# Q left unscaled before the score matmul, the scale inside the exponential, and the exponential's bias and the threshold made by one vector operation on two columns

## The chip, the cores and the metric

The kernel runs on one core of a Trainium2 chip. The metric is the device time of one execution in microseconds (us), the median of several runs; less is better. A core has TensorE (PE; PEld is its weight load), VectorE (DVE), ScalarE (ACT), GpSimd (POOL) and SyncE (SP), which issues most DMAs. Each engine takes its instructions in the order in which they are written and waits for others through semaphores.

## The reference

Sparse attention, then a layer of eight experts with one expert per token, then a dense layer with a gate:

```
scale = 1/sqrt(64);  scores = scale * q @ k.T           # 4 batches, 8 heads, 576 positions, 64 wide
thresh = max(scores) - tau                              # per query, tau = 0.02
scores = where(scores >= thresh, scores, -1e9)
attn = exp(scores - max(scores)); attn /= sum(attn) + 1e-9
x = (attn @ v), heads side by side                      # 2304 tokens x 512
e = argmax(x @ w_gate); x = gate * relu(x @ w1[e]) @ w2[e]
h = x @ w_in; out = (h * sigmoid(1.702 h)) @ w_out      # 512 -> 2048 -> 512
```

All tensors are float32.

## The kernel before, in words

**Stages.** Attention runs to about 303 us, the experts from there to 572 us, the dense layer to the end. In the last part of attention the expert with most tokens already starts on 256 tokens, which are known before the last queries are done.

**Attention.** The queries are cut into ten units: eight of 256 queries (two chunks of 128) and two "remainder" units of 2 x 64 queries of two batches. A tile is 128 queries by one head by 576 keys: 16 tiles in a full unit, 8 in a remainder unit, 144 in all. For each tile:

1. PE (`s_mm`, L360) multiplies Q by K. Both are float32 values split into a high part and a low part in the PE's reduced float format: Q as `qh` and `ql`, K as two halves of the 128 rows. The scores go to `pair`, two PSUM banks; there are three pairs. Columns 0 to 287 of both banks are used.
2. DVE (`red`, L370) makes the negated maximum `nm` of the 576 scores.
3. ACT (`thresh`, L374) makes the threshold `thr` = maximum - tau, one column.
4. ACT (`expo`, L378) makes `et` = exp(scores + nm).
5. DVE (`stt`, L389) makes `pt` = (scores >= thr) * et, with its row sum. This frees the pair.
6. PE transposes `pt` (L405; L416 for the remainder of the keys), ACT copies it to `ptT` (L411, L420), and PE multiplies it by V (L432, L442).

At the end of a unit, ACT copies its output to `aoT` (L451), PE brings it back and makes the router's logits (L478), DVE finds the maximum and its index (`lw`, `lg`, `mx`, `mi`), POOL makes the one-hot rows `oh` (L551, L553), PE counts with them (L602 to L605), and POOL scatters the tokens' numbers to their expert's table (L641).

**Q and K.** Q arrives by DMA as `qraw`. Apart from the first two of the 40 pieces, POOL handles each of its 38 pieces of 128 x 512 with three operations: it multiplies by the scale in place (`sc`, L306), makes `qh` (L318), and makes `ql` = Q - `qh` (L325). K goes through two (L282, L285), where one half of the rows gets the high part and the other the low part.

**Order.** The program is not written in a fixed order. Each piece of work is an `op` with an engine, a cost and a key (from the table `KEYS` and the tile's number); a planner (`Plan.order`) repeatedly takes the operation that can start first by its costs, the one with the lowest key among equals, and writes it out. So an edited operation, cost or key can reorder every engine.

**The first expert.** When unit 7 of 0 to 9 has been counted (the last of them that is needed for the 256 tokens), `pick_ops` finds the largest expert, SP reads its number into a register and loads its weights (`wraw`), POOL splits them (L770, L776), POOL gathers the 256 rows (L1229, `xg`), PE transposes these (L802), ACT and DVE split them (L807, L811), and PE starts on the expert (L1243).

## Time and profile before

| | us |
|---|---|
| timed runs | 977.53, 977.88, 980.33; median 977.88 |
| the profiled execution, whole | 984.31 |
| its span, first to last instruction | 982.6 |
| busy in the span: PE, DVE, ACT, POOL | 954.6, 562.9, 529.7, 411.2 |
| attention, to the first matmul of the first expert | 303.3 |
| experts, to the first matmul of the dense layer | 572.3 |

PE is busy for 97% of the span and its granted clock is 0.987 of full speed on average. A busy PE is not a PE at its peak: matmuls are pipelined, and a row's duration contains the pipeline's fill. So in the rows below the distance from one start to the next says more than the duration.

### The profile page before, as it was taken

Reading aid. Unit: us, or ns where it says so; the run is one execution under the profiler, and the core shown is the slowest. Engines: PE = TensorE matmul, PEld = TensorE weight load, DVE = VectorE, ACT = ScalarE, POOL = GpSimd, SP = SyncE. Lnnn points to the kernel's source line nnn. Section 1 sums busy time; section 2 is a strip of 40 time slices with the busy share of each in tenths; the row PEclk is TensorE's granted clock in tenths of the full one; section 3 lists DMA queues with packets and bytes.
Section 4 is the critical chain, followed back from the end, with each engine's and each line's share of the span. In section 5 each row is a group of like instructions: output and inputs, shape, how many; then the busy total and the mean of one; then the engine's idle time right before and its main releaser. Section 6 shows DMA issues by size and latency. Waiting matters only on the chain.

```text
span 982.6 us, 16924 instructions
## 1 busy us (share of the span) xinstructions
PE 954.6 (97%) x6204; PEld 864.9 (88%) x6205; DVE 562.9 (57%) x1189; ACT 529.7 (54%) x1170; POOL 411.2 (42%) x455
## 2 busy tenths in 40 slices
PE   7998999999989899999999999999999999999996
PEld 5888888888879899999999998999999999999995
DVE  6886888888856347888995488882411111111111
ACT  5886889889854345766675465543322322322221
POOL 6979978845275213555450000001432422522321
PEclk7999999999989999999999999999999999999999
DMA  8723532300243567877776373300200100000000
GB/s 309 223 88 109 162 108 79 108 22 22 58 137 108 171 197 217 257 214 235 241 223 212 116 220 86 106 24 13 95 22 1 54 11 1 33 0 1 33 1 33
DMA packets 50551, 106.90 MB, mean 109 GB/s; under 512 B 12816, under 2 KB 22032, under 8 KB 49936
## 3 DMA queue, kind: packets, MB, share of 16 engines
q1 hardware_dynamic: 45632, 93.43, 30.4%
q0 software_dynamic: 4096, 11.56, 3.8%
q8 instruction: 50, 0.82, 0.4%
q10 hardware_dynamic: 736, 0.79, 0.2%
q14 instruction: 37, 0.30, 0.1%
HBM read 87.37 MB, written 18.57 MB: 108 GB/s over the span
## 4 chain that ended last, share of the span: by engine, by line
PE 61%; DVE 2%; DMA 2%; issue 1%; ACT 0%; POOLq 0%; SPq 0%; DVEq 0%; ACTq 0%
PE b L1639 21%; PE b L1666 20%; PE b L1259 12%; PE b L1243 9%; DVE wlo L1393 1%; DMA wraw<-in_w 1%; PE b L1234 1%; DMA out<-xg,ids 1%; DVE hl L1250 0%; ACT whi L1389 0%; POOLq L1883 0%; DVE wil L1172 0%; ACT xg L1671 0%; ACT yt L1504 0%; ACT hh L1247 0%
## 5 line engine op out<-in xcount | busy, mean ns | idle before, releaser
L1648 DVE SCALAR_TENSOR_TENSOR th<-th,b 128x384 f32<-128x384 f32 x96 | 53.1, 553 | 250.1 <-ACT th L1644 250.1
L1644 ACT ACTIVATE th<-b 128x384 f32<-128x384 f32 x96 | 47.2, 492 | 201.9 <-PE b L1639 198.8
L1639 PE MATMUL b<-x2h,wil 128*128 128x384 f32 x384 | 129.5, 337 | 0.0
L1639 PE MATMUL b<-x2h,wih 128*128 128x384 f32 x384 | 129.3, 337 | 0.0
L1639 PE MATMUL b<-x2l,wih 128*128 128x384 f32 x384 | 128.9, 336 | 0.0
L370 DVE TENSOR_REDUCE nm<-pair 128x1 f32<-128x576 f32 x144 | 107.0, 753 | 27.8 <-PE pair L360 26.2
L389 DVE SCALAR_TENSOR_TENSOR pt<-pair,thr,et 128x576 f32<-128x576 f32 x144 | 114.3, 813 | 13.3 <-ACT et L378 12.3
L1659 POOL TENSOR_TENSOR gl<-th,gh 128x384 fp32r<-128x384 f32 x60 | 61.0, 1017 | 140.1 <-ACT gh L1656 136.3
L1666 PE MATMUL b<-woh,gl 128*128 128x512 f32 x276 | 109.2, 396 | 0.0
L1666 PE MATMUL b<-wol,gh 128*128 128x512 f32 x276 | 109.0, 395 | 0.0
L1666 PE MATMUL b<-woh,gh 128*128 128x512 f32 x276 | 107.3, 389 | 0.0
L378 ACT ACTIVATE et<-pair,nm 128x576 f32<-128x576 f32 x144 | 107.3, 745 | 0.0
L411 ACT COPY ptT<-bank 128x512 f32<-128x512 f32 x144 | 81.3, 589 | 25.4 <-PE bank L405 25.1
L1393 DVE TENSOR_TENSOR wlo<-wraw,whi 128x1024 fp32r<-128x1024 f32 x56 | 75.9, 1375 | 27.1 <-ACT whi L1389 24.1
L405 PE MATMUL bank<-ident,pt 128*128 128x128 f32 x576 | 86.1, 283 | 4.3 <-DVE pt L389 3.3
L1623 POOL TENSOR_TENSOR x2l<-xr,x2h 128x384 fp32r<-128x384 f32 x16 | 16.1, 1033 | 170.5 <-ACT x2h L1619 170.5
L360 PE MATMUL pair<-kst,qh 128*128 128x288 f32 x320 | 84.9, 348 | 1.3 <-DVE kst L285 0.6
L405 PEld LDWEIGHTS bank<-ident,pt 128*128 128x128 f32 x576 | 68.5, 145 | 17.3 <-ACT thr L374 6.2
L1639 PEld LDWEIGHTS b<-x2h,wih 128*128 128x128 f32 x384 | 72.2, 188 | 4.2 <-DVE th L1648 0.3
L1639 PEld LDWEIGHTS b<-x2l,wih 128*128 128x128 f32 x384 | 72.1, 188 | 3.9
L1639 PEld LDWEIGHTS b<-x2h,wil 128*128 128x128 f32 x384 | 72.0, 188 | 0.0
L1259 PE MATMUL b<-hh,whi 128*128 128x448 f32 (+6 forms) x224 | 71.4, 319 | 0.1
(256 smaller groups left out, 2309.6 us busy)
## 6 DMA issues: line engine op xcount, KB each, us to landing
wraw<-in_w SPq DMA_DIRECT2D x64, 512.0 KB, 4.7
qraw<-in_qd SPq DMA_DIRECT2D x40, 256.0 KB, 4.0
wiraw<-in_wi SPq DMA_DIRECT2D x32, 256.0 KB, 4.0
wraw<-in_wo SPq DMA_DIRECT2D x16, 512.0 KB, 3.6
kraw<-in_kd SPq DMA_DIRECT2D x14, 576.0 KB, 4.6
vt<-in_vf SPq DMA_DIRECT2D x4, 1024.0 KB, 7.6
xn<-xt SPq DMA_DIRECT2D x16, 256.0 KB, 3.2
xr<-x2t SPq DMA_DIRECT2D x20, 192.0 KB, 2.7
```

Of the source, the lines that this page charges most:

```text
L360: nc.tensor.matmul(s_ps[:, n, 0:288], w, ks[bb][:, h, 288 * n : 288 * n + 288], start=(i == 0), stop=(i == len(seq) - 1),)
L370: nc.vector.tensor_reduce(t["nm"], t["s"][:, :, 0:288], axis=AX.XY, op=ALU.max, negate=True)
L378: nc.scalar.activation(t["e"], t["s"][:, :, 0:288], AF.Exp, bias=t["nm"], scale=1.0)
L389: nc.vector.scalar_tensor_tensor(pt[:, 576 * x : 576 * x + 576].rearrange("p (n k) -> p n k", n=2), t["s"][:, :, 0:288], t["thr"][:, 0:1], ...
L405: nc.tensor.transpose(t["t"][:, c, :], pt[:, o : o + 128], ident)
L411: nc.scalar.copy(blk["ptT"][:, 4 * x : 4 * x + 4, 128 * ci : 128 * ci + 128], t["t"])
L1243: self.nc.tensor.matmul(h_ps, ww[:, o : o + 128], xx[dc], start=(k == 0), stop=(k == 11))
L1259: self.nc.tensor.matmul(y_ps, w[:, o : o + 128], h, start=(k == 0), stop=(k == 23))
L1393: nc.vector.tensor_tensor(w[1], self.raws.pop((r, which, k)), w[0].bitcast(F32), op=ALU.subtract)
L1639: self.nc.tensor.matmul(h_ps, w[:, dc, :], x[:, dc, :], start=(k == 0), stop=(k == 11))
L1659: eng.tensor_tensor(self.g[n][1], self.th.pop(n), self.g[n][0].bitcast(F32), op=ALU.subtract)
L1666: self.nc.tensor.matmul(o_ps, g[:, cs], w, start=(F == 0 and k == 0), stop=(F == 15 and k == 2))
```

## The change

Q is no longer multiplied by the scale 1/8. So the 38 operations `sc` on POOL go, and the scores in PSUM are eight times the reference's. The scale is put into the exponential: exp(scale * scores + bias), with bias = scale * `nm`. The threshold becomes maximum - 8 tau. Bias and threshold are now the two columns of one tile `thr`, made by one DVE operation per tile: (two constants) times `nm` plus (two constants). The first pair of constants, 1/8 and -1, stands in columns 500 and 501 of each PSUM pair, where no matmul writes; the second, `btadd`, in SBUF. ACT's operation `thresh` goes, and ACT's `expo` now waits for `thr` and not for `nm`. At the start DVE writes the constants (12 small operations in place of 2). The values in `KEYS` are different, so the planner writes another order.

```diff
 KEYS = dict(
-    KF=24.61, S=-3.65, R=61.35, X=43.87, TH=43.74, ST=85.35, T=-82.22, TE=40.03, TR=-1.15, TRE=-75.9, AV=1.41,
+    KF=-77.05, S=-4.92, R=-1.51, X=39.19, TH=-75.73, ST=24.75, T=-50.51, TE=74.0, TR=-50.68, TRE=-64.66, AV=0.13,
...
     def tau_prep():
         nc.vector.tensor_scalar(qscale, tau_sb, 0.0, float(D) ** -0.5, op0=ALU.is_ge, op1=ALU.mult)
-        nc.vector.scalar_tensor_tensor(ntau, tau_sb, -1.0, tau_sb, op0=ALU.mult, op1=ALU.min)
-
-    d_tau = pl.op("DVE", 0.3, -20, tau_prep, [dma(-200, 0.1, [tau_load])])
+        nc.vector.memset(btadd, 0.0)
+        nc.vector.tensor_scalar(ntau, tau_sb, 0.0, -3e38, op0=ALU.is_lt, op1=ALU.mult)
+        nc.vector.scalar_tensor_tensor(btadd[:, 1:2], tau_sb, -float(D) ** 0.5, ntau, op0=ALU.mult, op1=ALU.add)
+        for p in pairs:
+            nc.vector.memset(p[:, 0, 501:502], -1.0)
+            nc.vector.tensor_copy(p[:, 0, 500:501], qscale)
...
-        def sc():
-            q = qraws[ui][:, hs]
-            nc.gpsimd.tensor_scalar(q, q, qscale[:, 0:1], 0.0, op0=ALU.mult, op1=ALU.add)
...
             if fast:
-                nc.scalar.activation(h, q, AF.Copy, scale=qscale[:, 0:1])
-            elif pool:
+                nc.scalar.copy(h, q)
+            else:
                 nc.gpsimd.tensor_scalar(h, q, 1.0, 0.0, op0=ALU.mult, op1=ALU.add)
...
-        if pool:
-            o = pl.op("Pool", 0.7, key, sc, [o, d_tau])
...
     def thresh(t):
-        t["thr"] = sm_p.tile([128, 1], F32, name="thr")
-        nc.scalar.activation(t["thr"], t["nm"], AF.Identity, bias=ntau[:, 0:1], scale=-1.0)
+        t["thr"] = sm_p.tile([128, 2], F32, name="thr")
+        nc.vector.scalar_tensor_tensor(
+            t["thr"], t["s"][:, 0, 500:502], t["nm"][:, 0:1], btadd, op0=ALU.mult, op1=ALU.add
+        )
 
     def expo(t):
         t["e"] = e_p.tile([128, 2, 288], F32, name="et")
-        nc.scalar.activation(t["e"], t["s"][:, :, 0:288], AF.Exp, bias=t["nm"], scale=1.0)
+        nc.scalar.activation(t["e"], t["s"][:, :, 0:288], AF.Exp, bias=t["thr"][:, 0:1], scale=qscale[:, 0:1])
...
-                x = pl.op("ACT", 0.63, n + K["X"], lambda t=t: expo(t), [r], take=("e", te))
-                th = pl.op("ACT", 0.19, n + K["TH"], lambda t=t: thresh(t), [r])
-                deps = [x, th]
+                th = pl.op("DVE", 0.16, n + K["TH"], lambda t=t: thresh(t), [r, d_tau])
+                x = pl.op("ACT", 0.63, n + K["X"], lambda t=t: expo(t), [th], take=("e", te))
+                deps = [x]
```

What the planner makes of it is shown at three places. The first is POOL where unit 1 ends (about 80 to 89 us before). Before, with `oh` the one-hot rows for which PE waits:

```order
L306 TENSOR_SCALAR qraw<-qraw,qscale 128x512 x2
L318 TENSOR_SCALAR qh<-qraw 128x512 x2
L325 TENSOR_TENSOR ql<-qraw,qh 128x512 x2
L306 TENSOR_SCALAR qraw<-qraw,qscale 128x512 x5
L551 CAST ef<-mi 128x2
L553 TENSOR_SCALAR oh<-shc,ef 128x8 x2
```

And POOL there in the changed kernel (its line numbers are 2 lower in this part; L289 and L292 are the two operations on K):

```order
L289 TENSOR_SCALAR kst<-kraw,half 128x1152 x2
L292 TENSOR_TENSOR kst<-kraw,kst 128x1152 x2
L321 TENSOR_SCALAR qh<-qraw 128x512
L289 TENSOR_SCALAR kst<-kraw,half 128x1152
L325 TENSOR_TENSOR ql<-qraw,qh 128x512
L549 CAST ef<-mi 128x2
L551 TENSOR_SCALAR oh<-shc,ef 128x8 x2
```

The five scalings of Q that stood ahead of `oh` are gone; pieces of K for a later batch stand there in their place.

The second place is PE in the last units, where the first gathered rows are transposed (L802). Before, in the middle of the last unit's scores:

```order
L360 MATMUL pair_147<-kst,qh 128x288 x2
L360 MATMUL pair_147<-kst,ql 128x288 x2
L802 MATMUL bank_150<-ident,xg 128x128 x4
L405 MATMUL bank_149<-ident,pt 128x128 x4
L360 MATMUL pair_146<-kst,qh 128x288 x2
L360 MATMUL pair_146<-kst,ql 128x288 x2
```

In the changed kernel (L800 there), with the last products with V (L430, L440) and the first expert's matmul (L1241) around it:

```order
L800 MATMUL bank_149<-ident,xg 128x128 x4
L800 MATMUL bank_150<-ident,xg 128x128 x4
L476 MATMUL pair_146<-iw,aoT 128x144
L430 MATMUL pair_148<-ptT,vt 64x64 x8
L440 MATMUL pair_148<-ptT,vt_1429 128x64
L430 MATMUL pair_148<-ptT,vt 64x64 x8
L440 MATMUL pair_148<-ptT,vt_2234 128x64
L1241 MATMUL bank_149<-kraw,qraw 128x256 x12
```

Both transposes now stand behind all scores, a few matmuls ahead of the expert that reads them.

The third place is DVE in the steady part of attention. Before, with `pt` the masking of a tile:

```order
L370 TENSOR_REDUCE nm<-pair_147 128x1
L370 TENSOR_REDUCE nm<-pair_146 128x1
L389 SCALAR_TENSOR_TENSOR pt,sums<-pair_147,thr,et 128x576
L370 TENSOR_REDUCE nm<-pair_148 128x1
L370 TENSOR_REDUCE nm<-pair_147 128x1
L389 SCALAR_TENSOR_TENSOR pt,sums<-pair_146,thr,et 128x576
```

And in the changed kernel (L366 is the maximum there, L370 the new operation, L387 the masking):

```order
L366 TENSOR_REDUCE nm<-pair_148 128x1
L370 SCALAR_TENSOR_TENSOR thr<-pair_148,nm,btadd 128x2
L387 SCALAR_TENSOR_TENSOR pt,sums<-pair_146,thr,et 128x576
L387 SCALAR_TENSOR_TENSOR pt,sums<-pair_148,thr,et 128x576
L366 TENSOR_REDUCE nm<-pair_146 128x1
L366 TENSOR_REDUCE nm<-pair_147 128x1
L370 SCALAR_TENSOR_TENSOR thr<-pair_146,nm,btadd 128x2
L370 SCALAR_TENSOR_TENSOR thr<-pair_147,nm,btadd 128x2
```

One small operation per tile joins the two large ones, often right behind the maximum that it reads. Behind attention, the rows of PE, DVE, ACT and POOL are the same in both kernels, one for one; only some of SP's loads change places.

## Rows read from the trace of the kernel before

**Rows 1.** Stretches: length, busy of PE, PEld, DVE, ACT, POOL; clock, DMA, GB/s.
```profile
80.00:104.00 24.00, 21.08 (x246) 19.51 (x245) 15.11 (x41) 15.48 (x42) 22.68 (x28) 0.93 0.45 126
104.00:262.00 158.00, 157.39 (x1244) 131.05 (x1244) 138.98 (x348) 141.45 (x354) 108.04 (x139) 1.00 0.23 76
262.00:303.00 41.00, 37.02 (x363) 32.78 (x361) 28.34 (x61) 26.52 (x65) 26.12 (x24) 0.92 0.46 135
331.00:572.00 241.00, 237.78 (x1619) 233.42 (x1620) 173.03 (x310) 140.15 (x275) 83.71 (x85) 1.00 0.68 211
```

**Rows 2.** The chain that ended last: start, length, what.
```profile
331.27 2.27 PE b L1243 x14
...
572.29 8.32 PE b L1639 x48
```

**Rows 3.** Groups by line, 0 to 300 us: busy, mean ns | idle before, releaser.
```profile
L370 DVE TENSOR_REDUCE nm<-pair 128x1 f32<-128x576 f32 x144 | 107.0, 753 | 27.8 <-PE pair L360 26.2
...
L325 POOL TENSOR_TENSOR ql<-qraw,qh 128x512 fp32r<-128x512 f32 x38 | 48.1, 1276 | 0.2
L374 ACT ACTIVATE thr<-nm,ntau 128x1 f32<-128x1 f32 x144 | 44.5, 309 | 7.7 <-DVE nm L370 7.5
L285 POOL TENSOR_TENSOR kst<-kraw,kst 128x1152 fp32r<-128x1152 f32 (+1 forms) x15 | 38.5, 2569 | 0.0
...
L306 POOL TENSOR_SCALAR qraw<-qraw,qscale 128x512 f32<-128x512 f32 x38 | 25.9, 688 | 10.0 <-DMA qraw<-in_qd 9.8
L318 POOL TENSOR_SCALAR qh<-qraw 128x512 fp32r<-128x512 f32 x38 | 23.3, 622 | 6.9 <-PE pair L360 6.7
...
L282 POOL TENSOR_SCALAR kst<-kraw,half 128x1152 fp32r<-128x1152 f32 (+1 forms) x15 | 17.9, 1196 | 2.9 <-PE pair L360 2.4 <-DMA kraw<-in_kd 0.4
```

**Rows 4.** The same view, 104 to 262 us alone.
```profile
L374 ACT ACTIVATE thr<-nm,ntau 128x1 f32<-128x1 f32 x87 | 27.0, 311 | 1.0 <-DVE nm L370 0.9
```

**Rows 5.** Waits of the weight loads, 104 to 262 us: total, times, longest.
```profile
PEld bank L405 <- ACT thr L374: 4.2, 11, 0.4
```

**Rows 6.** Order of time on DVE: start, length, instruction; small operations on PSUM.
```profile
294.19 0.15 DVE L622 SCALAR_TENSOR_TENSOR rj<-bank,oh 128x8 f32<-128x8 f32 x1
...
294.27 0.16 DVE L622 SCALAR_TENSOR_TENSOR rj<-bank,oh 128x8 f32<-128x8 f32 x1
```

**Rows 7.** Order of time on POOL, the end of unit 1.
```profile
83.73 2.69 POOL L306 TENSOR_SCALAR qraw<-qraw,qscale 128x512 f32<-128x512 f32 x4
87.17 0.69 POOL L306 TENSOR_SCALAR qraw<-qraw,qscale 128x512 f32<-128x512 f32 x1 [0.74 <-DMA qraw<-in_qd]
```

**Rows 8.** Order of time on PE, the same place.
```profile
88.45 0.17 PE L602 MATMUL pair<-oh,tri 128*128 128x8 bf16 x1 [1.90 <-POOL oh L553]
```

**Rows 9.** Stretches behind two waits of PE, columns as in Rows 1.
```profile
88.45:94.25 5.80, 5.71 (x60) 5.49 (x59) 3.45 (x11) 0.93 (x4) 5.52 (x10) 0.71 0.28 99
279.25:285.80 6.55, 6.55 (x33) 5.18 (x35) 3.01 (x6) 2.92 (x6) 6.47 (x4) 0.56 0.37 113
```

**Rows 10.** Order of time on POOL: the first gather for the first expert.
```profile
274.39 1.02 POOL L1229 DMA_INDIRECT xg<-xn,itf  x1 [0.16 <-issue]
```

**Rows 11.** Order of time on PE around their transposes.
```profile
275.07 0.43 PE L360 MATMUL pair<-kst,ql 128*128 128x288 f32 x2
279.25 1.09 PE L802 MATMUL bank<-ident,xg 128*128 128x128 f32 x4 [3.75 <-DMA xg<-xn,itf]
...
301.70 0.61 PE L802 MATMUL bank<-ident,xg 128*128 128x128 f32 x4
```

**Rows 12.** Order of time on DVE, the first expert's second weights.
```profile
295.15 1.22 DVE L776 TENSOR_TENSOR kst<-wraw,kst 128x1024 fp32r<-128x1024 f32 x1
...
297.48 5.35 DVE L776 TENSOR_TENSOR kst<-wraw,kst 128x1024 fp32r<-128x1024 f32 x1 [0.36 <-ACT kst L772]
```

**Rows 13.** Order of time on POOL, beside the second of these.
```profile
299.38 2.35 POOL L776 TENSOR_TENSOR kst<-wraw,kst 128x1024 fp32r<-128x1024 f32 x1
```

**Rows 14.** Order of time on DVE, the first tiles.
```profile
9.66 1.18 DVE L327 SCALAR_TENSOR_TENSOR ql<-qraw,qscale,qh 128x512 fp32r<-128x512 f32 x1
```

More of the change, by code (lines that the diff above doesn't have):

```diff
@@ L182 @@
 KEYS = dict(
-    KF=24.61, S=-3.65, R=61.35, X=43.87, TH=43.74, ST=85.35, T=-82.22, TE=40.03, TR=-1.15, TRE=-75.9, AV=1.41,
-    OE=49.75, L=-76.58, F=53.56, FR=-35.48, FX=62.99, FS=16.49, K=28.16, Q=59.94, LD=11.03, P=22.54,
+    KF=-77.05, S=-4.92, R=-1.51, X=39.19, TH=-75.73, ST=24.75, T=-50.51, TE=74.0, TR=-50.68, TRE=-64.66, AV=0.13,
+    OE=71.86, L=6.66, F=85.05, FR=-35.13, FX=18.93, FS=77.49, K=49.92, Q=72.42, LD=20.32, P=109.57,
 )
@@ L263, in tau_prep @@
         nc.vector.tensor_scalar(qscale, tau_sb, 0.0, float(D) ** -0.5, op0=ALU.is_ge, op1=ALU.mult)
-        nc.vector.scalar_tensor_tensor(ntau, tau_sb, -1.0, tau_sb, op0=ALU.mult, op1=ALU.min)
-    d_tau = pl.op("DVE", 0.3, -20, tau_prep, [dma(-200, 0.1, [tau_load])])
+        nc.vector.memset(btadd, 0.0)
[4 more added lines that the diff above has]
+            nc.vector.tensor_copy(p[:, 0, 500:501], qscale)
+    btadd = cst.tile([128, 2], F32, name="btadd")
+    d_tau = pl.op("DVE", 1.2, -20, tau_prep, [dma(-200, 0.1, [tau_load])])
     def k_ops(b, h0, n, after, fast, key, first=None):
@@ L315, in hi @@
             if fast:
-                nc.scalar.activation(h, q, AF.Copy, scale=qscale[:, 0:1])
-            elif pool:
+                nc.scalar.copy(h, q)
+            else:
                 nc.gpsimd.tensor_scalar(h, q, 1.0, 0.0, op0=ALU.mult, op1=ALU.add)
-            else:
-                nc.gpsimd.tensor_scalar(h, q, qscale[:, 0:1], 0.0, op0=ALU.mult, op1=ALU.add)
         def lo():
             q, h, l = qraws[ui][:, hs], qs[ui][0][:, hs].bitcast(F32), qs[ui][1][:, hs]
-            if pool:
-                nc.gpsimd.tensor_tensor(l, q, h, op=ALU.subtract)
-            else:
-                nc.vector.scalar_tensor_tensor(l, q, qscale[:, 0:1], h, op0=ALU.mult, op1=ALU.subtract)
+            (nc.gpsimd if pool else nc.vector).tensor_tensor(l, q, h, op=ALU.subtract)
         pool = not fast and QPOOL[ui]
         o = dma(key + K["LD"] if first is None else first, 0.9, [load], after_raw)
-        if pool:
-            o = pl.op("Pool", 0.7, key, sc, [o, d_tau])
-        o = pl.op("ACT" if fast else "Pool", 0.6 if fast else 0.63, key, hi, [o, d_tau] + after_q)
+        o = pl.op("ACT" if fast else "Pool", 0.6 if fast else 0.63, key, hi, [o] + after_q)
         qop[(ui, g)] = pl.op("Pool" if pool else "DVE", 1.3 if pool else 0.68, key, lo, [o])
@@ L391, in stt @@
             t["s"][:, :, 0:288],
-            t["thr"][:, 0:1],
+            t["thr"][:, 1:2],
             t["e"],
```

## The prediction

> **What bounds the kernel now.** I read the page first (PE busy 97%, no other engine above 58%), then the chain of waits, the stretches, the groups by line, the waits, and last the order of time at the places where PE stood still. In the chain the reader is to see that from 331 us to the end it runs through PE matmuls with few other steps [rows 2], and the stretch to 572 us has PE busy for 237.8 of 241 us [rows 1]. The change leaves the order of PE, DVE, ACT and POOL behind attention as it was. So whatever attention gains or loses should come out at the end nearly one for one, and the question is how long attention takes.
>
> Attention has two kinds of stretches. From 104 to 262 us PE is busy for 157.4 of 158 us at full clock, beside an ACT that is busy for 141.5 and a DVE for 139.0 [rows 1]: PE is the bound, though not by much. From 80 to 104 us and from 262 to 303 us PE is idle for 2.9 and 4.0 us, and its granted clock is 0.93 and 0.92 [rows 1]. There the time is lost to single waits.
>
> **The change part by part.**
>
> *The threshold off ACT.* It removes 144 operations on ACT, busy for 44.5 us in all [rows 3]. PE bounds the long stretch, so this is worth only what PE waits for there. PE's idle time there is 0.6 us [rows 1]; the weight loads name an ACT threshold as the releaser for 4.2 us [rows 5], most of which lies beside matmuls still running. The gain is thus between 0 and 4.2 us.
>
> *One operation more per tile on DVE.* The trace has no such operation. The nearest is `rj`, also a scalar-tensor-tensor operation on a few PSUM columns: 0.15 to 0.16 us, and the next DVE operation starts 0.08 us after it started [rows 6]. From above I take the threshold on ACT, 0.309 us [rows 3], for the case that it is held up behind the maximum that it reads. The 158 us hold 87 of the 144 thresholds [rows 3, 4]. With 0.08 us DVE's 139.0 us become 146.0; with 0.16 us, 152.9; both less than 158, so PE stays the bound and the cost is nothing. With 0.309 us they become 165.9, 7.9 us over, and over all 144 tiles 7.9 x 144/87 = 13.1 us. I take 0.16 us, the row that is nearest in kind.
>
> For the steady part, gain and cost together, I take -1.5 us: near the 0.6 us of idle time in 158, a little more because ACT has 87 x 0.309 = 27 us less to do there, and the range is -4.2 to +13.1.
>
> *The scaling of Q off POOL.* It removes 38 operations of 0.688 us, 25.9 us [rows 3]. POOL is not the bound, but at one place PE waits for it: at 88.45 us PE has waited 1.90 us for the one-hot rows of unit 1 [rows 8], and these stand on POOL behind five scalings that begin at 83.73 and, with a wait for the last one's DMA, end at 87.86 [rows 7]. These are exactly the operations that go. Behind that wait PE's granted clock is 0.71 for 5.80 us [rows 9]: 5.80 x 0.29 = 1.7 us. I take both: -3.6 us.
> What is late next there: in the new order two high and two low parts of K, a piece of Q and one more high part of K stand ahead of the one-hot rows, 3 x 1.20 + 2 x 2.57 + 0.62 + 1.28 = about 10.6 us [rows 3], and with the one-hot rows themselves, by their time now, 11.5. They may start when the last scores of batch 0 are done. In PE's new order about 15 us of work (my count at the durations of such groups in the trace) stand between those scores and the count. That covers it by 3.5 us; if POOL comes late to that point, up to the 3.6 us return.
>
> *The transposes of the gathered rows.* PE ends its scores at 275.5 us and waits 3.75 us, until 279.25, for the first gather [rows 11], which POOL began at 274.39 [rows 10]. The granted clock is then 0.56 for 6.55 us [rows 9]: 6.55 x 0.44 = 2.9 us. In the new order both transposes stand behind all scores, as the second one does already now, at 301.70, with no wait [rows 11]. So the first wait goes with its slow clock: -6.65 us. It costs nothing that they come later as long as the split of the gathered rows is done in time. PE has about 2 us of work between the second transpose and the expert, and the split takes about as long.
>
> *The tail.* The split of the gathered rows stands on DVE behind the low part of the expert's second weights. That operation takes 1.22 us at one time and 5.35 us at another [rows 12], and the long one ends, at 302.83, only behind its neighbour on POOL, which ends at 301.73 [rows 13]. Before, PE was busy elsewhere during it. Now it would lie ahead of the split, and the loss is between 0 and 4.1 us. I take +1.0: it depends on which POOL operation stands beside it, and POOL's order there has gaps. The Trainium skill ("GPSIMD Engine Reference", section "1. Specifications") says that POOL's SBUF interfaces are shared with DVE, with contention for DVE operations with two SBUF inputs, as this one is. By that rule the loss is the full 4.1 us whenever POOL is at work, and the sum would be 3.1 us higher.
>
> *The start.* DVE writes 10 more constants between 3 and 5 us, while it waits for K. Then the first exponential has to wait for `thr`, which stands behind a low part of Q of 1.18 us [rows 14], and three thresholds join the maxima ahead of the first masking: 3 x 0.16 = +0.5 us (0 to 1.2).
>
> *The sum.* -1.5 - 3.6 - 6.65 + 1.0 + 0.5 = -10.25 us. The profiled execution took 984.31 us whole, 1.7 more than its span, and would take 974.1. The median of the timed runs is 977.88, 6.4 less than that execution; for the timed runs I predict 977.88 - 10.25 = 967.6 us.
>
> **The rivals.**
>
> *DVE becomes the bound in the steady part.* DVE reaches PE's 158 us when the operation takes (158 - 139)/87 = 0.22 us per tile, and the kernel gets slower than before from 0.28 us, where the loss of 8.75 us over 144 tiles eats the other terms. At 0.309 us: -10.25 + 1.5 + 13.1 = +4.4, 982.2 us. For it: it reads what the operation just ahead writes, DVE is already at 88%, and every wait of an engine at 97% is passed on. Against it: [rows 6], and other work often stands between the two. 11%.
>
> *The waits come back elsewhere.* POOL reaches the one-hot rows late (+3.6), or DVE's low part of the weights delays the expert (+3.1 beyond the 1.0), or another wait of a few us with its slow clock appears in the new order of the last units, for example because the first expert's weights, which start with the count of unit 7, now have six tiles fewer of PE's work before they are needed. Two of these: about +8, 975.6 us. For it: the old order too was a planner's, and had such waits. Against it: the loads of these weights have over 10 us to spare before. 20%.
>
> *PE gets all it can.* The steady part gives the whole 4.2 us, the tail and the start cost nothing: -14.45, 963.4 us. For it: ACT loses a fifth of its work. Against it: PE idles for 0.6 us only. 7%.
>
> **How the numbers follow.** The forecast, 967.6 us, has 62%, with a range of its own of 963 to 973. About 0.3%, 2.9 us, is what a measurement of this kernel can tell from no change: 975.0 to 980.8 counts as the same. Faster: 58 of the forecast's 62, 7 of the third rival, 7 of the second's 20, together 0.72. The same: 4 of the forecast, 11 of the second, 1 of the first, 0.16. Slower: 10 of the first, 2 of the second, 0.12. The range that should hold the time 8 times in 10 is 959.5 to 978.5: it takes in the second and the third rival, and leaves out the first and a little at the bottom.
>
> **What the new profile would show.** Right: no wait of PE over 1 us at the end of unit 1 and none at the transposes; a granted clock of 1.00 in the stretches that hold them; first expert matmul at about 293 us; a unit of 16 tiles at 29 us or a little less; the new operation at 0.15 to 0.17 us; DVE at about 96% in the steady part. Wrong: PE idle in the steady part with DVE's masking or ACT's exponential as the releaser (the first rival); PE waiting for the one-hot rows, for the split of the gathered rows or for the first expert's weights (the second); or attention shorter by 10 us and the end not, which would mean that the experts' loads and not attention set the time.

## The result, and the profile after

The changed kernel takes 988.20 us, median of 6 runs (987.02 to 989.26), beside 981.08 us for the kernel before on the same chip (977.53 to 982.78): ratio 1.0074, 95% interval 1.0046 to 1.0103. It is 7.1 us slower; forecast were 10.25 us less. The two profiled executions, 988.62 and 984.31 us, differ by 4.3 us only, since that of before was a long one. A second profiled execution took 979.76 us (before) and 990.29 us (after).

Where the difference lies is read off the same events in the traces (us, differences worked out from them; the last three columns are the second executions):

| from | to | before | after | difference | before, 2nd | after, 2nd | difference |
|---|---|---|---|---|---|---|---|
| start of the span | 57th masking | 125.5 | 122.2 | -3.3 | 122.7 | 122.5 | -0.2 |
| 57th masking | 129th masking (72 tiles of the steady part) | 130.5 | 135.1 | +4.6 | 130.5 | 135.2 | +4.7 |
| 129th masking | last masking | 40.4 | 31.0 | -9.3 | 39.0 | 31.0 | -7.9 |
| last masking | first matmul of the first expert | 7.0 | 15.6 | +8.6 | 7.0 | 18.9 | +11.8 |
| first expert | first matmul of the dense layer | 268.8 | 273.4 | +4.6 | 268.4 | 271.6 | +3.1 |
| dense layer | end | 410.5 | 409.5 | -1.0 | 410.5 | 409.5 | -0.9 |

In the new order the last masking stands earlier, so its two rows are read together: from the 129th masking to the first expert the time is 0.7 us shorter in the first pair and 3.9 longer in the second. In both pairs the steady part and the experts are longer. So the waits that should go did go, and other stages give back more. The stretches after, to be laid beside [rows 1] (same columns):

```profile
80.00:104.00 24.00, 22.84 (x273) 21.21 (x273) 20.73 (x61) 17.92 (x39) 23.55 (x25) 1.00 0.59 194
104.00:262.00 158.00, 154.96 (x1205) 126.57 (x1203) 145.02 (x405) 133.94 (x256) 86.91 (x107) 1.00 0.20 59
262.00:303.00 41.00, 37.22 (x366) 32.32 (x364) 27.23 (x90) 27.20 (x59) 25.07 (x31) 0.96 0.42 117
331.00:572.00 241.00, 236.77 (x1583) 231.46 (x1584) 173.27 (x310) 138.78 (x274) 86.67 (x85) 0.99 0.67 207
```

From 80 to 104 us PE has 22.84 us for 21.08, at full clock (the second execution of before has 21.68 there, at full clock too). But from 104 to 262 us PE is idle for 3.0 us where it was 0.6, with no engine at its limit: DVE is busy for 145.0 of 158 us (92%, not the 96% expected). The groups of the tile's operations from 0 to 300 us (line, operation, count, busy, mean ns, idle before and its releaser):

```profile
L376 ACT ACTIVATE et<-pair,thr,qscale 128x576 f32<-128x576 f32 x144 | 118.3, 834 | 22.0 <-DVE thr L370 18.1
L387 DVE SCALAR_TENSOR_TENSOR pt<-pair,thr,et 128x576 f32<-128x576 f32 x144 | 116.7, 815 | 12.0 <-ACT et L376 8.5
L366 DVE TENSOR_REDUCE nm<-pair 128x1 f32<-128x576 f32 x144 | 106.9, 751 | 7.1 <-PE pair L356 7.0
```

and, for the exponential, its instructions before and the new operation's after (minimum, median and maximum in ns):

```profile
L378 ACT ACTIVATE et<-pair,nm x144: 718/747/787, 9.5 to 295.3; 128x576 f32<-128x576 f32 x144
```

```profile
L370 DVE SCALAR_TENSOR_TENSOR thr<-pair,nm,btadd x144: 177/215/221, 10.6 to 287.1; 128x2 f32<-128x2 f32 x144
```

The exponential now takes 834 ns on average and 832 in the median, where it took 745 and 747: nothing in the prediction speaks of that. ACT waits 18.1 us for the threshold before it. The new operation takes 0.214 us, not the 0.16 taken from [rows 6].

At the transposes [rows 11] the picture on PE is this (start, length, what, idle time before and releaser):

```profile
292.18 0.41 PE L476 MATMUL pair<-iw,aoT 128*128 128x144 f32 x2
295.83 0.17 PE L600 MATMUL pair<-oh,tri 128*128 128x8 bf16 x1 [3.24 <-POOL oh L551]
...
300.94 1.04 PE L800 MATMUL bank<-ident,xg 128*128 128x128 f32 x8
...
304.00 0.72 PE L1241 MATMUL bank<-kraw,qraw 128*128 128x256 f32 x4
```

The transposes at 300.94 wait for nothing, as forecast. But PE stands still for 3.24 us at 295.83, for unit 8's one-hot rows, and its granted clock is 0.57 behind that; the first expert starts at 304.00 and not at 293. On POOL (same columns) the one-hot rows stand behind two low parts of the expert's weights:

```profile
290.59 2.34 POOL L774 TENSOR_TENSOR qraw<-wraw,qraw 128x1024 fp32r<-128x1024 f32 x1
292.90 2.33 POOL L774 TENSOR_TENSOR qh<-wraw,qh 128x1024 fp32r<-128x1024 f32 x1
295.18 0.18 POOL L549 CAST ef<-mi 128x2 f32<-128x2 uint32 x1
295.46 0.60 POOL L551 TENSOR_SCALAR oh<-shc,ef 128x8 bf16<-128x8 f32 x2
```

A third loss follows in the experts. Three of DVE's operations of the routing (start, length, what), which took 0.58, 0.17 and 0.21 us before:

```profile
307.14 1.90 DVE L554 TENSOR_TENSOR ld<-lg,mx 128x8 f32<-128x8 f32 x1
...
312.12 1.28 DVE L1095 TENSOR_TENSOR rest<-n,shc 128x8 f32<-128x8 f32 x1
...
314.04 1.99 DVE L1108 TENSOR_TENSOR before<-shc,n 128x64 f32<-128x64 f32 x1
```

Each ends within 0.1 us of an operation of POOL on the weights (309.01, 313.38 and 315.95 us). The second expert's positions and rows come later, and PE waits 1.37 us for them at 333.04, with a clock of 0.56 behind it:

```profile
333.04 0.73 PE L1232 MATMUL bank<-ident,xg 128*128 128x128 f32 x4 [1.37 <-DMA xg<-xn,it]
```

```profile
295.83:299.80 3.97, 3.87 (x35) 3.36 (x35) 0.31 (x5) 2.20 (x4) 3.89 (x8) 0.57 0.53 159
334.40:341.00 6.60, 6.60 (x28) 6.60 (x29) 4.13 (x6) 3.59 (x5) 4.74 (x3) 0.56 0.45 97
```

### The profile page after: what moved, and what is told of

It is laid out like the page before. It is cut to its first block, busy times and chain, and to the rows that moved or that the text cites. A ratio compares the mean times of both kernels' runs of the same rounds, so it can differ in the third digit from the quotient of the medians.

```text
span 987.0 us, 16922 instructions
## 1 busy us (share of the span) xinstructions
PE 955.9 (97%) x6204; PEld 862.1 (87%) x6205; DVE 585.0 (59%) x1341; ACT 523.6 (53%) x1026; POOL 387.6 (39%) x417
## 4 chain that ended last, share of the span: by engine, by line
PE 59%; DVE 3%; DMA 2%; ACT 1%; issue 1%; POOL 1%; POOLq 0%; DVEq 0%; ACTq 0%
PE b L1637 20%; PE b L1664 19%; PE b L1241 9%; PE b L1257 9%; DVE wlo L1391 2%; PE b L1232 1%; DMA wiraw<-in_wi 1%; DMA wraw<-in_w 1%; DMA out<-xg,ids 1%; ACT whi L1387 0%; DVE hl L1248 0%; POOL cv_lf L1163 0%; DVE cv_t L1155 0%; POOL cv_lf L1164 0%; DVE cv_t L1151 0%
## 5 line engine op out<-in xcount | busy, mean ns | idle before, releaser
L376 ACT ACTIVATE et<-pair,thr,qscale 128x576 f32<-128x576 f32 x144 | 118.3, 834 | 22.0 <-DVE thr L370 18.1
L387 DVE SCALAR_TENSOR_TENSOR pt<-pair,thr,et 128x576 f32<-128x576 f32 x144 | 116.7, 815 | 12.0 <-ACT et L376 8.5
L366 DVE TENSOR_REDUCE nm<-pair 128x1 f32<-128x576 f32 x144 | 106.9, 751 | 7.1 <-PE pair L356 7.0
L403 PE MATMUL bank<-ident,pt 128*128 128x128 f32 x576 | 89.4, 282 | 6.7 <-ACT ptT L418 2.7
L403 PEld LDWEIGHTS bank<-ident,pt 128*128 128x128 f32 x576 | 65.9, 143 | 24.3 <-ACT ptT L409 7.1
L356 PE MATMUL pair<-kst,qh 128*128 128x288 f32 x320 | 81.5, 336 | 3.6 <-POOL kst L292 1.4
L1241 PE MATMUL b<-xh,whi 128*128 128x448 f32 (+6 forms) x224 | 70.1, 313 | 1.9 <-DVE hl L1248 1.9
## 6 DMA issues: line engine op xcount, KB each, us to landing
kraw<-in_kd SPq DMA_DIRECT2D x14, 576.0 KB, 4.8
```

Of the source, the lines that this page charges most:

```text
L356: nc.tensor.matmul(s_ps[:, n, 0:288], w, ks[bb][:, h, 288 * n : 288 * n + 288], start=(i == 0), stop=(i == len(seq) - 1),)
L366: nc.vector.tensor_reduce(t["nm"], t["s"][:, :, 0:288], axis=AX.XY, op=ALU.max, negate=True)
L376: nc.scalar.activation(t["e"], t["s"][:, :, 0:288], AF.Exp, bias=t["thr"][:, 0:1], scale=qscale[:, 0:1])
L387: nc.vector.scalar_tensor_tensor(pt[:, 576 * x : 576 * x + 576].rearrange("p (n k) -> p n k", n=2), t["s"][:, :, 0:288], t["thr"][:, 1:2], ...
L403: nc.tensor.transpose(t["t"][:, c, :], pt[:, o : o + 128], ident)
L1241: self.nc.tensor.matmul(h_ps, ww[:, o : o + 128], xx[dc], start=(k == 0), stop=(k == 11))
```

## The experiments

"Own order" below means that every engine's instructions stand as in the kernel named, apart from the edit: the planner's costs and keys are left alone. In b and i the edit goes through the planner, and some neighbouring instructions of the last units move with it. A unit is 16 tiles, a quarter of the time from the 57th to the 121st masking. Times in us, exp and threshold as means; the ratio is to before, in the same session (its medians there: 981.4 for the first four, 981.0, 980.3 and 981.7 for the next four, four and three).

| kernel | exp | threshold | unit | first expert | dense | median | ratio (95%) |
|---|---|---|---|---|---|---|---|
| before | .745 | .309 ACT | 29.11 | 303.3 | 572.1 | 981.1 | 1 |
| after | .834 | .214 DVE | 30.00 | 304.0 | 577.4 | 988.2 | 1.0074 (1.0046 to 1.0103) |
| a_const_scale | .745 | .216 DVE | 29.40 | 302.1 | 573.3 | 984.5 | 1.0032 (1.0014 to 1.0051) |
| b_oh_dve | .834 | .216 DVE | 29.99 | 305.8 | 578.4 | 988.7 | 1.0073 (1.0042 to 1.0104) |
| c_thr_act | .741 | .303 ACT | 29.84 | 305.4 | 576.3 | 986.7 | 1.0060 (1.0041 to 1.0079) |
| d_thr_dve | .742 | .212 DVE | 32.34 | 320.0 | 590.9 | 1001.9 | 1.0219 (1.0185 to 1.0254) |
| e_oh_first | .835 | .214 DVE | 30.00 | 304.7 | 576.0 | 987.3 | 1.0059 (1.0036 to 1.0082) |
| f_both | .744 | .214 DVE | 29.40 | 297.9 | 570.9 | 983.7 | 1.0026 (1.0006 to 1.0046) |
| g_no_sc | .744 | .309 ACT | 29.11 | 296.8 | 564.6 | 978.8 | 0.9972 (0.9952 to 0.9992) |
| h_no_thr | .749 | none | 29.01 | | | 1312.7 | one run, attention alone is read |
| i_xtr_late | .745 | .309 ACT | 29.11 | 296.9 | 564.1 | 977.7 | 0.9971 (0.9953 to 0.9988) |
| j_low_dve | .745 | .216 DVE | 29.40 | 298.7 | 573.0 | 983.6 | 1.0028 (1.0008 to 1.0048) |
| k_thr_sbuf | .744 | .751 DVE | 37.77 | 373.8 | 641.9 | 1051.9 | 1.0735 (1.0697 to 1.0773) |
| l_thr_dve_sbuf | .758 | .207 DVE | 29.04 | 298.4 | 568.5 | 982.0 | 1.0020 (0.9999 to 1.0040) |
| m_best | .745 | .309 ACT | 29.12 | 299.0 | 568.3 | 980.6 | 0.9986 (0.9968 to 1.0004) |

**The steady part.** Three kernels first: the constant scale, and two with the threshold on the other engine (the edits are abridged here and below).

```
a: expo   ... bias=t["thr"][:, 0:1], scale=qscale[:, 0:1]   ->   scale=0.125
c: thresh   DVE operation -> nc.scalar.activation(thr[:, 1:2], nm, Identity, bias=btadd[:, 1:2], scale=-1.0)
   expo     bias=nm, scale=0.125
d: before; thresh   ACT operation -> nc.vector.scalar_tensor_tensor(thr, s[:, 0, 501:502], nm, ntau, mult, add);   -1 in column 501 of each pair
```

> The changed kernel with the exponential's scale as the constant 0.125 and not from a column of a tile; every engine's order is as in the changed kernel. Three theories on the steady part, where a unit of 16 tiles takes 30.0 us against 29.1 before. T1, the exponential (0.834 us in the changed kernel against 0.745 before) sets it: the exponential falls to about 0.745, a unit to 29.1 to 29.3 us, the kernel is 5 to 7 us faster than the changed one, 981 to 983 us. T2, the new DVE operation (0.214 us) between maximum and exponential sets it: the exponential falls, but a unit stays at 29.8 us or more and the kernel gains less than 2 us. T3, the order from the new table of numbers sets it: as T2.

> The changed kernel, in its own order, with the threshold computed on ACT as before, the exponential's bias taken from the maximum itself and its scale the constant 0.125, so that operations and dependencies of a tile are those of before. T1 and T2: a unit takes 29.1 to 29.4 us, the kernel is 5 to 7 us faster than the changed one, 981 to 983 us. T3, the order: a unit stays at 29.8 to 30.2 us, the kernel within 2 us of the changed one. T1 against T2 is read from this run beside the one with the constant scale: T1 has both alike, T2 has only this one faster.

> The kernel before, in its own order, with the threshold (one column) computed on DVE by the new kind of operation at the moment where ACT computed it; the exponential still depends on the maximum alone, with the constant scale. T2: DVE's operation of 0.21 us lengthens the unit from 29.1 to about 30.0 us and the kernel by 5 to 6 us, to 987 us. T1 and T3: a unit stays at 29.1 us, and the kernel within 2 us of before (981 us), or up to 2 us faster, since ACT has a fifth less to do.

The constant scale (a) gives the exponential its 0.745 us back, and two thirds of the unit's loss, 30.00 to 29.40 us; the kernel is 3.7 us faster than the changed one. So T1 holds for 0.60 us of the 0.89. The exponential in a:

```profile
L376 ACT ACTIVATE et<-pair,thr x144: 721/743/794, 11.3 to 284.3; 128x576 f32<-128x576 f32 x144
```

The rest is less plain. With the threshold on ACT again (c) a unit of the new order takes 29.84 us: T3's figure, though T3 had no gain in a. With the threshold on DVE (d) one of the old order takes 32.34: T2's sign, at more than three times its size. In d the waits of ACT from 140 to 260 us (total, times, longest) are led by

```profile
ACT et L378 <- DVE thr L374: 22.2, 37, 1.1
```

although the exponential there takes nothing that the threshold writes. The threshold's operation reads a column of one of the two PSUM banks from which the exponential reads its scores, and by the profile the exponential starts when DVE's semaphore tells that this operation is done. Two more kernels separate DVE's time from that wait: h leaves the threshold out (from a, the bias is the maximum itself), and l takes d but computes it from the maximum in SBUF.

```
h: thresh   (none);   stt   t["thr"][:, 1:2] -> btadd[:, 1:2];   expo   bias=nm, scale=0.125
l: before; thresh   -> nc.vector.tensor_scalar(thr, nm, -1.0, ntau, mult, add)
```

> The changed kernel in its own order with the exponential's scale constant and its bias the maximum itself, and the threshold left out: the masking compares with one constant for all rows (so rows may go to other experts, and the attention stage alone is read). With the constant scale a unit took 29.40 us, before 29.11. If the DVE operation is what is left of the difference, a unit takes 29.1 us or less; if the new order is, it stays at 29.4.

> The kernel before, in its own order, with the threshold on DVE from the maximum in SBUF alone (one input, two scalar operands, nothing read from PSUM). With the operation that reads PSUM, a unit took 32.34 us and the exponentials named the threshold as their releaser. If that came from the exponential waiting for an operation that reads its scores' bank: a unit falls to 29.1 to 29.6 us and the kernel to 981 to 985 us. If it came from DVE's additional work in an order not made for it: a unit stays at 32 us, the kernel at 1000 us.

Without the threshold a unit takes 29.01 us in the new order, so that order by itself costs the steady part nothing. In l a unit takes 29.04 us: an operation of 0.21 us more on DVE per tile costs nothing there, and no wait of an exponential for the threshold is left. The four units from the 57th to the 121st masking, columns as in [rows 1], in before, after, c, h and l:

```profile
125.48:241.91 116.43, 116.35 (x917) 96.72 (x916) 102.77 (x252) 104.42 (x261) 81.38 (x105) 1.00 0.21 68
122.23:242.24 120.01, 118.10 (x919) 96.34 (x917) 112.64 (x316) 102.07 (x197) 62.13 (x79) 1.00 0.18 59
123.14:242.49 119.35, 117.89 (x917) 96.19 (x916) 102.94 (x253) 105.29 (x260) 61.78 (x79) 1.00 0.18 59
118.56:234.61 116.05, 115.92 (x918) 96.43 (x917) 102.69 (x252) 96.23 (x196) 61.70 (x79) 1.00 0.20 63
121.00:237.16 116.16, 115.66 (x919) 96.77 (x917) 109.66 (x317) 94.95 (x197) 81.54 (x105) 1.00 0.22 69
```

DVE is as full in l (109.7 of 116.2 us, 94%) as in the changed kernel (112.6 of 120.0), and yet its unit is the shorter one. In the changed kernel PE's idle time, 1.9 us for 0.1, is only half of the 3.6 us that the four units lose; the other half lies inside rows that count as busy.

So in the changed kernel the exponential's length costs 0.60 us a unit and the new operation 0.39; since DVE's time alone cost nothing in l, I put the 0.39 down to the exponential that stands behind it. From 120 to 240 us the exponentials in kernel a wait 6.5 us for the threshold, those in h 2.4 us for the maximum. But in the new order the wait was not tried apart from DVE's time, so the cause of the 0.39 is argued and not shown. The threshold on ACT costs 0.83 us a unit in the new order (c beside h), which was not made for it. In the old order l, which has it off ACT, is 0.07 us a unit faster than before, and the 29.01 of h is 0.10 below before: as far as these runs show, there was not more to win there.

Why the columns lie in PSUM was a question by itself:

```
k: a; thresh   t["s"][:, 0, 500:502] -> pcol   (the same two constants, in SBUF)
```

> The changed kernel with the constant scale (984.5 us), in the same order, with the new operation's two constant columns in SBUF and not in PSUM, so that all its inputs come from SBUF. If DVE is held up by POOL when it reads two inputs from SBUF: the operation takes 0.4 us or more on average and up to 2.5 us at worst, a unit 31 us or more, the kernel 12 us or more longer. If not: the operation takes 0.2 us or less, a unit 29.4 us, the kernel 984 to 985 us.

```profile
L370 DVE SCALAR_TENSOR_TENSOR thr<-pcol,nm,btadd x144: 179/221/10755, 10.7 to 353.6; 128x2 f32<-128x2 f32 x144
```

The median is the same, but 37 of the 144 take over 0.4 us, up to 10.76. The one that starts at 194.99 ends at 205.55 us, and POOL works without a gap from before it until 205.54, on eight operations from SBUF to SBUF. The Trainium skill ("SBUF — State Buffer", section "Who interferes with whom") says that a DVE instruction with two SBUF inputs contends with a GpSimd instruction that reads SBUF, that the ports they share are an exclusive lock, and that the order of issue decides who blocks. The trace agrees, and goes further: the wait lasts through the whole row of POOL's operations. With 37.77 us a unit this is what the form of the change avoids.

**The tail.** b makes unit 8's one-hot rows on DVE; e and f (which is e with a's constant) put them ahead of the two low parts on POOL.

```
b: oneh   small -> nc.vector if ui == 8 else small;   op("Pool", ...) -> op("DVE", ...) for it
e: split.lo   for (0, 1) and (0, 2): written out behind the one-hot rows of unit 8
```

> The changed kernel with the one-hot rows of the ninth unit made on DVE and not on POOL, where they stand behind two low parts of the first expert's weights of 2.3 us each. The tail theory: the wait of 3.24 us of PE at 295.83 us goes, and with it most of the slow clock behind it (0.57 for 3.97 us, 1.7 us); the first expert's matmuls start at about 299 us and not at 304.0, and the end comes 4 to 5 us earlier, about 983.5 us. The rival: the experts are held by their loads or by DVE's operations that are slow beside POOL, and the end moves by less than 1.5 us, to 987 us or more.

> The changed kernel with one exchange on POOL: the one-hot rows of the ninth unit (1.0 us) stand ahead of the two low parts of the first expert's weights (2.3 us each) and not behind them. The making of the rows on DVE had moved nothing, since DVE's copy took 5.07 us beside these two low parts. If these operations, in POOL's queue or beside DVE, are what PE waits for: the 3.24 us wait goes and most of the slow clock behind it, the first expert's matmuls start at about 299 us and not 304.0, the kernel takes 983 to 984 us. If the experts' positions and weights hold the end anyway, the expert starts earlier but the dense stage does not, and the kernel takes 987 us or more.

> The changed kernel with both edits: the exponential's scale a constant, and the one-hot rows of the ninth unit ahead of the two low parts on POOL. If the two losses are separate, their gains add: 3.7 us of the constant scale (measured) and 4 to 5 us of the exchange, 979.5 to 980.5 us, below before's 981.4. If the end is held by the experts' loads: 984 us, as with the constant scale alone.

b is no faster. DVE's copy of two numbers per row for the one-hot rows (DVE, then POOL; start, length, what):

```profile
290.54 5.07 DVE L549 CAST ef<-mi 128x2 f32<-128x2 uint32 x1
```

```profile
290.95 2.33 POOL L774 TENSOR_TENSOR qraw<-wraw,qraw 128x1024 fp32r<-128x1024 f32 x1
293.25 2.33 POOL L774 TENSOR_TENSOR qh<-wraw,qh 128x1024 fp32r<-128x1024 f32 x1
```

5.07 us, to the end of the second low part: leaving POOL's queue does not help while POOL runs. In e and f the rows come early and the 3.24 us wait goes. In e PE then waits 2.70 us at the transposes and starts the expert no earlier (304.7). In f the expert starts 4.2 us earlier than in a, the dense layer 2.4, and the median is lower by 0.8 (the profiled execution of f, 982.2 us, was the shortest of its twelve). In time both kernels come out as in the second case of their expectation, 987.3 and 983.7 us; what holds them was only supposed there. What the experts wait for in f is DVE, 1.39 us at 305.67 and 1.83 at 312.08, and j tests why.

```
j: f; split.lo   (nc.gpsimd if pool ...) -> (nc.gpsimd if pool and which == 0 ...)
```

> The changed kernel with the constant scale and the one-hot rows ahead of the low parts (983.7 us), and in addition the two low parts of the first expert's second weights computed on DVE (1.2 us each) and not on POOL (2.4 us each), at the same place of the order. If the operations of the routing on DVE (one of 1.90 and one of 1.99 us in the changed kernel, 0.17 to 0.58 before) are long because POOL's low parts run beside them: they fall to 0.2 to 0.6 us, PE's waits in the first expert (1.8, 1.5 and 1.4 us) shrink, and the kernel is 2 to 3 us faster, 981 us. If they are long for another reason: they stay above 1 us and the kernel stays within 1 us of 983.7.

The same operations in f and in j (DVE):

```profile
302.39 2.62 DVE L584 TENSOR_TENSOR rg<-rec,gs 128x8 f32<-128x8 f32 x1
...
306.83 1.66 DVE L1093 SCALAR_TENSOR_TENSOR n<-n,shc 128x8 f32<-128x8 f32 x1
...
308.73 2.31 DVE L1097 TENSOR_TENSOR ge<-shc,rest 128x72 f32<-128x72 f32 x1
```

```profile
305.46 0.17 DVE L584 TENSOR_TENSOR rg<-rec,gs 128x8 f32<-128x8 f32 x1
...
308.83 0.17 DVE L1093 SCALAR_TENSOR_TENSOR n<-n,shc 128x8 f32<-128x8 f32 x1
...
309.23 0.23 DVE L1097 TENSOR_TENSOR ge<-shc,rest 128x72 f32<-128x72 f32 x1
```

2.62, 1.66 and 2.31 us become 0.17, 0.17 and 0.23: POOL's low parts had held them. PE's two waits for DVE are gone too, and the second expert's first matmul comes at 328.2 us and not at 329.5. But the time did not follow, 983.6 beside 983.7 us. The next rows of j show where it went (ACT, DVE, PE):

```profile
340.77 1.05 ACT L1387 CAST whi<-wraw 128x1024 fp32r<-128x1024 f32 x1 [4.27 <-DMA wraw<-in_w]
341.85 1.23 DVE L1391 TENSOR_TENSOR wlo<-wraw,whi 128x1024 fp32r<-128x1024 f32 x1 [4.84 <-ACT whi L1387]
342.99 1.23 DVE L1248 SCALAR_TENSOR_TENSOR hl<-b,hh 128x304 fp32r<-128x304 f32 x3
343.51 2.65 PE L1241 MATMUL b<-kraw,ql 128*128 128x304 f32 x9 [2.46 <-DVE hl L1248]
```

PE waits 2.46 us for a split of the hidden layer, which stands on ACT and DVE behind weights whose DMA has just landed. In f the same cast starts at 340.51, behind a wait of 2.94 us, and PE's wait is 1.13: j comes earlier and waits longer, and over the 6 us behind it the clock is 0.72 in j and 1.00 in f. So the mechanism is shown; what it costs the kernel is not, since at 343 us a load of weights sets the time in both.

**Q and the transposes by themselves.**

```
g: before; sc   nc.gpsimd.tensor_scalar(q, q, qscale ...) -> pass;   expo   scale=1.0 -> 0.125;   ntau x 8
i: g; the planner's latency of the gather, 4.0 -> 8.0
m: i; e's exchange, for the last low part (0, 3) of the first weights
```

> The kernel before, in its own order, with Q unscaled and the scale as the constant 0.125 in the exponential: the 38 scalings on POOL are gone and nothing else moves (the bias is the unscaled maximum, which cancels in the normalization). The prediction's second term by itself: PE's wait of 1.90 us for the one-hot rows of unit 1 and the slow clock behind it go, the kernel is 3.6 us faster than before, 977.5 to 978 us. The rival, that something else is late at the same place or behind it: 980.5 to 982 us.

> The kernel before, in its own order, with Q unscaled and the scale as a constant in the exponential (978.8 us), and the first transposes of the gathered rows moved behind some 7 us of other work of PE. The prediction's third term by itself: PE's wait for the gather (3.4 us in that kernel) and the slow clock behind it go; 5 to 6.5 us faster, 972 to 974 us. The rival, that the waits turn up again before the experts or in them: less than 2 us faster, 977 to 979 us.

> The kernel with Q unscaled, the constant scale and the late first transposes (977.7 us), in which PE waits 1.98 us for the ninth unit's one-hot rows and then runs at a clock of 0.57 for 7.15 us; here those rows stand on POOL ahead of the last low part of the first expert's first weights and not behind it. If the waits at this end of attention are worth what the prediction's third term says once nothing takes their place: 2.0 + 7.15 x 0.43 = 5 us faster, 972 to 973.5 us. If a next wait takes the place again: 976.5 us or more.

g removes the wait of [rows 8] and the slow clock behind it, and reaches the 57th masking at 120.4 us instead of 125.5 or 122.7; the median falls by 2.2 us. Theory and rival both have part: the wait went, 60% of its price came. In the second execution of the kernel before, PE waits 1.26 us there, and the clock behind it is 1.00 (columns of the second line as in [rows 1]):

```profile
87.22 0.17 PE L602 MATMUL pair<-oh,tri 128*128 128x8 bf16 x1 [1.26 <-POOL oh L553]
```

```profile
87.22:93.02 5.80, 5.71 (x71) 5.29 (x70) 4.01 (x12) 2.99 (x8) 5.52 (x10) 1.00 0.29 107
```

In l, which has the same order on POOL, PE waits 1.64 us there and the clock behind it is 1.00 as well: the 1.7 us of slow clock belonged to one execution.

In i the wait for the gather (3.44 us in g) is gone, but the median is 977.7 beside 978.8 us, and the two ratios to before are alike: the rival. PE in g, i and m:

```profile
273.87 0.63 PE L802 MATMUL bank<-ident,xg 128*128 128x128 f32 x4 [3.44 <-DMA xg<-xn,itf]
```

```profile
278.04 0.60 PE L802 MATMUL bank<-ident,xg 128*128 128x128 f32 x4
...
282.85 0.17 PE L602 MATMUL bank<-oh,tri 128*128 128x8 bf16 x1 [1.98 <-POOL oh L553]
```

```profile
284.20 0.69 PE L432 MATMUL bank<-ptT,vt 128*64 128x64 f32 x16 [1.21 <-DVE rj L622]
...
286.85 1.12 PE L432 MATMUL pair<-ptT,vt 128*64 128x64 f32 x16 [0.62 <-DVE pt L389]
...
290.20 1.11 PE L405 MATMUL bank<-ident,pt 128*128 128x128 f32 x4 [1.60 <-ACT aoT L451]
```

Take away the first wait and PE waits 1.98 us for the one-hot rows; take that away too (m), and it waits at three places, while DVE's low part of the second weights takes 4.44 us:

```profile
290.01 4.44 DVE L776 TENSOR_TENSOR kst<-wraw,kst 128x1024 fp32r<-128x1024 f32 x1 [2.48 <-ACT kst L772]
```

The first expert starts at 296.8, 296.9 and 299.0 us; m had lost 1.9 us to i by the 57th masking, and from the 129th masking to the first expert the three take 45.9, 46.3 and 46.5 us. From 276 to 297 us POOL is busy for 19.9 of 21 us in i and for 19.7 in m, with splits, one-hot rows and scatters: the wait moved, it did not go. g and i are 0.3% faster than the kernel before, with intervals clear of 1, and so faster than the changed one; which of the two is the better is not settled (978.8 and 977.7).

**The experts stage.** A second execution of each kernel:

> The changed kernel itself, a second look. If the longer experts stage belongs to the change's order: again 272 to 275 us from the first expert's first matmul to the first of the dense stage. If it varies from execution to execution: another value, 268 to 272 us.

> The kernel before itself, a second look. If the stage belongs to the order: again 268 to 270 us from the first expert's first matmul to the first of the dense stage. If it varies: 270 us or more, or below 267 us.

From the first expert to the dense layer the changed kernel took 273.4 and 271.6 us, the kernel before 268.8 and 268.4. That of before is as the first theory has it, that of after a little under its 272 to 275: some 3 us belong to the order, and up to 2 vary between executions. Of the other kernels (h apart, whose rows go to other experts) those in the new order have 271 to 274 us, k alone 268, those in the old order 267 to 271. Two of the 3 us can be placed: from the first expert's first matmul to the second's, all seven traces of the old order have 27.8 to 27.9 us, and those of the new one 28.7 to 31.6 (30.4 and 30.0 in the changed kernel). There the new order has POOL's two low parts of the second weights (306.59 and 313.46 us in the changed kernel) beside the routing on DVE, where the old one has one (304.89 in before). j, which moves them to DVE, still has 29.5, so they are not the whole of it, and what else makes the difference stays open.

## Why the prediction was wrong

10.25 us less were forecast and 7.1 more were measured, 17.4 us apart. By an estimate from the runs some 9.5 of them are the first step below; the rest lies at the end of attention and in the experts, and the two pairs of executions do not agree on the shares.

- **The threshold off ACT and one operation more on DVE** (forecast -1.5 us, range -4.2 to +13.1). This step failed. The steady part lost 0.89 us a unit, 4.6 us over the 72 tiles of the table; at 0.89 a unit all 144 tiles lose 8.0 (an estimate). That lies in the step's range, but in the part that it had kept for a DVE with no time left, and DVE's time was free (l). The gain was as small as forecast: 0.07 to 0.10 a unit, 0.6 to 0.9 us in all. But the step did not ask what the exponential becomes. It counted one operation more on DVE, and gave the exponential its old price in its old place. Two things were missing. Its scale, now read from a column, makes it 89 ns longer: 0.60 a unit, shown by a, 5.4 us over nine units. And it now stands behind the new operation: 0.39 a unit, 3.5 us, with the cause argued. The Trainium skill ("ScalarE: Activation LUTs", section "What ACT_TABLE_LOAD costs") has the price: about 93 ns for each operand of an activation that is a pointer to a column. The trace agrees: 834 - 745 = 89 ns. Nor did ACT have 27 us less to do for 87 thresholds [rows 4]. A unit holds 26.1 us of ACT in before and 23.7 in l, 26.3 in c and 24.1 in h: 0.14 to 0.15 us per threshold, not the 0.309 of a row.
- **The first rival** had the place but not the mechanism: it made DVE the bound from 0.22 us per operation. The operation took 0.214 and DVE stayed at 92% (its busy time grew by 0.11 us per operation in l); the loss came from the length of the exponential and, it seems, of the chain from maximum to masking, of which a share of busy time says nothing. Its 982.2 us were 6 too low.
- **Q's scaling off POOL** (-3.6): right in kind, too large. No wait of PE over 1 us is left at unit 1's end, and the clock is 1.00. Alone it brings 2.2 us (0.8 to 4.7 by its interval). In the first row of the table it is mixed with the tiles up to the 57th, which are longer after the change.
- **The transposes** (-6.65): the wait went and its price did not come. The step named the transposes as the only thing late, and looked for the split of the gathered rows behind them; it did not follow POOL's queue to unit 8's one-hot rows, which the new order puts behind two low parts of 2.3 us (a wait of 3.24 us and a clock of 0.57 behind it). The second rival had it in general ("another wait of a few us with its slow clock appears in the new order of the last units"), at 20%; e, i and m show that in this stretch a next wait was there each time.
- **The tail** (+1.0, range 0 to 4.1, from [rows 12, 13]): mis-sized. The prediction weighed a rule of the Trainium skill ("GPSIMD Engine Reference", section "1. Specifications") that POOL's SBUF interfaces are shared with DVE, and took it for one operation alone. The trace agrees with it at small operations of the routing with two inputs in SBUF as well: 1.90, 1.28 and 1.99 us. The copy of 5.07 us in b has one input only. By the table, the way from the 129th masking to the first expert is 0.7 us shorter or 3.9 longer, and the experts are longer by 3.1 to 4.6 us; not all of this is contention.
- **The path behind attention** (at nothing). The prediction took it that what attention gains or loses comes out at the end nearly one for one. It does not: the experts took 3.1 to 4.6 us more, and in f and j time gained ahead of the second expert was in part lost behind it.
- **The start** (+0.5): 12.1 became 12.3 us at the first masking (11.6 and 12.3 in the second executions); right within what two executions differ. DVE writes ten small operations there in place of two, so eight more; the description of the change has twelve, and the prediction ten more.
- **The base.** The forecast stood on 977.88 us, the median of three runs; over six it is 981.08, so 3.2 us of the distance from 967.6 to 988.2 belong to the base. And the slow clocks of 1.7 and 2.9 us in [rows 9] were read from one execution that was 4.5 us longer than the next. There the first is gone, and the second is 0.74 over 6.55 us behind a wait of 3.51; in d it is 1.00 behind a wait of 3.35. A price that hangs on a single execution's clock needs a second one.

## What to carry to other kernels

When an edit gives an operation a new operand, price that operation anew, and not only the ones that are added or removed: a constant that becomes a column, or an input from an operation further down the chain, can cost on every tile (here 0.60 us a unit for the column). Busy shares do not show what a tile waits for: with the same threshold a unit took 29.04, 29.11, 29.40, 29.84, 32.34 or 37.77 us, depending on its engine, its operands, the order and what stands behind it, and 29.01 without it. And before a wait is counted as gone, walk each engine's queue from there to the next thing that all of them must finish: in the last 30 us of attention the waits removed in e, i and m were replaced by others.

## What the runs showed of the hardware

- An exponential of 128 x 576 from PSUM: 745 ns with a constant scale, 834 ns with the scale from a column, in the same order (a and after).
- Small DVE operations with all tensor inputs in SBUF (128x2 to 128x72), most of which take 0.17 to 0.23 us where POOL does not hold them, took 1.28 to 10.76 us where POOL worked from SBUF to SBUF beside them, through up to eight POOL operations on end, not one. The threshold with one tensor input from PSUM kept to 0.221 us at most in 144 (after).
- One operation of 0.21 us more per tile took 0.11 us more of DVE's time (l), and a threshold of 0.309 us 0.14 to 0.15 us of ACT's: the rows of neighbours on an engine overlap, so a row was longer than the busy time that it added.
- An exponential on ACT was held until a DVE operation had read one column of a PSUM bank that both read (22.2 us in 120 in d), though it used nothing from it; with the DVE operation reading SBUF alone (l) that wait was gone. By the profile it is a wait for DVE's semaphore; who put it there no run shows.
- A wait of PE of 1.90 us was followed by a clock of 0.71 over 5.8 us, one of 1.26 us at the same place in another execution of the same kernel by 1.00.
